# A gated mix of memory attention and FFN: the order of all five engines written in the source

## The chip, the cores and the metric

The kernel runs on one core of a Trainium2 chip. The metric is the time of one execution in microseconds on the device. The engines are named PE (TensorE), ACT (ScalarE), DVE (VectorE), POOL (GpSimd) and SP (SyncE, which here only starts transfers and signals).

## The reference

x is 2048 rows of 640 in float32. Attention has 32 heads of 20 channels and goes over four segments ("chunks") of 512 rows; from chunk to chunk it carries a memory M and its normaliser z. Beside it stands a gated FFN of width 1728, and a gate per row mixes the two.

```python
for s in range(4):
    logits = einsum("bhqd,bhkd->bhqk", qs, ks) * scale + causal_mask
    a_dot  = softmax(logits) @ vs
    pq     = phi(qs)                      # phi(t) = t + 1 if t > 0 else exp(t)
    a_mem  = (pq @ M) / (pq @ z + 1e-6)
    outs.append(g * a_mem + (1 - g) * a_dot)      # g = sigmoid(beta), per head
    M, z   = M + phi(ks).T @ vs, z + sum(phi(ks))
a = concat(outs) @ wo
b = (silu(x @ w1) * (x @ w3)) @ w2
out = sigmoid(x . gate_w) * a + (1 - sigmoid(x . gate_w)) * b
```

## The kernel before

Each float32 operand of a large product is split into a rounded high part and a low remainder, and a product is made of three passes (high by high, high by low, low by high). The split is a cast on ACT and a subtraction on POOL or DVE (`split`, L128; from PSUM `split_psum`, L326).

PE's work is a stream of *works* (`Work`, L132): the projections q, k, v (`q0_2` is chunk 0, block 2), the FFN's gate and up products g and u, its down product f (`f0_13_1_0`: chunk 0, group that begins with block 13, rows 1, columns 0), the output projection op, and the works of the memory: pkt (transposes of phi(k)), pm (the update of M), nd (the read). Every work is cut into two halves of its contraction, 64 rows each, that run on the two row halves of PE; the first halves form one stream and the second halves another, and `step` (L281) writes matmuls of the two alternately. The second half of a work starts behind a `nop` on SP that waits for its first half (`one`, L194, the wait is put down to L204). A work takes one of eight PSUM banks, and its `evac` writes the steps that empty the bank and go on from there.

Between these works the writer sets attention's steps, on slots (`attention`, L1042): `s_unit` (L850; scores, and their row maximum on DVE at L869), `max_rows` (L873), `t_unit` (L887; shifted scores, the exponential on ACT at L901, a triangle on POOL at L904) and `pv_quad` (L909). Tiles s, t, P and o belong to these.

The writer counts estimated PE time per half (`clocks`) and uses it for two things only: which half goes next, and when a bank is taken to be free again: a fixed `hold` after the work's last matmul (`close_work`, L189). A few steps are set by fixed distances: the transposes of phi(k) 3.4 us after their k work, the update of M 1.9 us after those (L663, L679). The FFN's down product may start as soon as the Python list `hts` has its inputs, which is when the chain's code was written, not when it is done.

The FFN's chain: g is read by a tanh on ACT (L757) and a product on DVE (L758); u by a product on DVE (L775); then ht is cast on ACT and its remainder taken on POOL (both in `split`, L129 and L130). f's result is folded into acc by ACT for the first group (L807) and by DVE afterwards (L809). Weights W come in by SP's DMA (L369) into raw tiles wr, a number of steps later their split is written (`w_split`, L373); its cast is pinned behind an exponential. X of chunks 2 and 3 is split by `split_x` (L478). oT is the transposed attention output, split for op (`part`, L1073).

Only PE and SP take the order of the source. The instructions of ACT, DVE and POOL are ordered by the framework's scheduler, which runs its own model of time, except where `here` keeps program order and `behind` pins an instruction behind another.

Of the kernel before, what the change touches and what calls it, by code (L numbers as in the profile page):

```python
# [18 lines left out]
P = 128  # L19
# [10 lines left out]
NP, AGE = 2, 4  # L30
# [7 lines left out]
STEP = 700  # L38


@with_exitstack
def gated_mix(ctx: ExitStack, tc: tile.TileContext, xT, wqk, wv, w13, w2, w2h, wo, beta, out):
# [40 lines left out]
    def gates():  # L83
        here(nc.sync.dma_start(gH, beta.rearrange("(o h) -> o h", o=1).broadcast_to([P, H])))
        for i in range(4):
            here(nc.sync.dma_start(cR[i::4], beta.rearrange("(h o) -> h o", o=1)))
        for g in (gH, cR):
            here(nc.scalar.activation(g, g, AF.Exp, scale=-1.0))
            here(nc.vector.tensor_scalar(g, g, 1.0, None, op0=ALU.add))

        nc.vector.reciprocal(cR, cR)
        nc.vector.tensor_scalar(cR, cR, -1.0, 1.0, op0=ALU.mult, op1=ALU.add)
# [16 lines left out]
    here = tc.keep_in_program_order  # L109
    last = {}  # L110

    def behind(ins):

        def pin(i):
            if ins is not None:
                tc.add_manual_dep(i.ins, ins.ins.name,
                                  mybir.DependencyInfo(mybir.DependencyClass.NoSync, mybir.DependencyReason.DATA),
                                  reason="behind")
            return i
        return pin  # L120
# [7 lines left out]
    def split(dst, src, lo=None, pin=lambda ins: ins):  # L128
        pin(nc.scalar.copy(dst[:, 0], src))  # L129
        (lo or nc.gpsimd.tensor_sub)(dst[:, 1], src, dst[:, 0].bitcast(F32))  # L130

    class Work:  # L132

        def __init__(self, name, parts, evac, hold, old=None, olds=None, ready=None):
            self.ready = ready
            self.name, self.parts, self.evac, self.hold, self.old, self.olds = name, parts, evac, hold, old, olds or {}
# [10 lines left out]
    def bank_tile(name, hold=1500):  # L147
# [28 lines left out]
    def open_work(w):  # L176

        k = until.index(min(until))
        until[k] = float("inf")
        w.bank = k  # L180
# [8 lines left out]
    def close_work(w):  # L189

        until[w.bank] = max(clocks) + w.hold
        w.evac(w.ps)
# [51 lines left out]
    def events():  # L244

        while dense["ns"] >= dense["hook"]:
            dense["hook"] += STEP
            stores()
            w_step()
            for f in on_step:  # L250
                f()
        for e in list(timed):
            if dense["ns"] >= e[0] and len(under) < 2 and len(behind_one) < 3:
# [63 lines left out]
    def finish_all():  # L317

        while flight[0] is not None or behind_one or under or timed or waiting:
            if flight[0] is None and behind_one:  # L320
                dense["n0"] += APART
            if step(None) is None:
                dense["ns"] += STEP
                events()

    def split_psum(dst, src, name, pin=lambda ins: ins):  # L326

        hi = bank_tile(name, 1800)[:, :src.shape[-1]]
        pin(nc.scalar.copy(dst[:, 0], src))
        nc.scalar.copy(hi, dst[:, 0].bitcast(F32))  # L330
        nc.vector.tensor_sub(dst[:, 1], src, hi)
# [27 lines left out]
    def w_load():  # L359
# [10 lines left out]
        raws.append([k, raw, n, clock["step"], None])  # L370
        clock["next"] += 1

    def w_split():  # L373
        k, raw, n, _, after = raws.pop(0)
        assert k < clock["oldest"] + NW
        w = sp.tile([P, 2, D + 2], FR, tag="W", name=f"W{k}", bufs=NW)
        tiles[k] = w
        if k not in EARLY:
            freed.append(clock["step"])
        split(w[:, :, :n], raw[:, :n], lo=nc.vector.tensor_sub if k < 7 else None, pin=behind(after))  # L380

    def w_step():


        clock["step"] += 1
        for r in raws:
            if clock["step"] - r[3] == (AGE // 2 if "exp" in last else 2 * AGE) and r[0] >= 7:
                r[4] = last.get("exp", last["act"])
# [3 lines left out]
        elif raws and raws[0][0] < clock["oldest"] + NW and \  # L392
                clock["step"] - raws[0][3] >= (AGE if "exp" in last or raws[0][0] < 7 else 2 * AGE + 1):
# [6 lines left out]
    def w_get(i):  # L400

        while i not in tiles:
            if not raws or raws[-1][0] < i and len(raws) < NRAW:
# [10 lines left out]
    def load_first(c):  # L414
# [21 lines left out]
        def hi(dst, src):  # L436
            last["act"] = here(nc.scalar.copy(dst[:, 0], src))
# [18 lines left out]
    def load_wide(c):  # L456
        for _ in EARLY:
            w_load()
        for kb in range(KB):
            split(Xs[c][:, :, kb, :], xraw[c][:, kb], lo=nc.vector.tensor_sub if kb % 2 else None)  # L460
# [17 lines left out]
    def split_x(c):  # L478
        x_tile(c)
        for kb in range(KB):  # L480
            split_psum(Xs[c][:, :, kb, :], xraw[c][kb], f"xh{c}_{kb}", here)
# [28 lines left out]
    def parts(name, ps, phi=None):  # L510


        s = ht_tile([P, 2, L], FR, name)
        last["act"] = nc.scalar.copy(s[:, 0], ps)
        if phi is not None:
            e = f_tile("phi_t")
            last["act"] = nc.scalar.activation(e, ps, AF.Relu, scale=-1.0)
            last["act"] = nc.scalar.activation(e, e, AF.Exp, scale=-1.0)
        nc.vector.tensor_sub(s[:, 1], ps, s[:, 0].bitcast(F32))
        if phi is not None:  # L520
            nc.vector.scalar_tensor_tensor(phi, ps, 0.0, e, op0=ALU.max, op1=ALU.add)
        return s
# [20 lines left out]
    def q_block(c, mb, i, alloc, oldest=None):  # L543

        def evac(ps):
            if c and mb == 0:
                big["q", c] = alloc(f"pq{c}")
            s = parts(f"qs{c}_{mb}", ps, big["q", c][:, mb * L:(mb + 1) * L] if c else None)
            store_parts(0, c, mb, s)
            q_done.add((c, mb))  # L550

        yield Work(f"q{c}_{mb}", proj(w_get(i), Xs[c]), evac, 2200, i if oldest is None else oldest)
# [805 lines left out]
```

## Time and profile before

| | us |
|---|---|
| median of three runs | 1167.65 (1167.01 to 1170.57) |
| the profiled run | 1166.93 |
| its span, first to last instruction | 1165.2 |
| PE busy | 1113.2 (96%) |
| DVE busy | 584.9 (50%) |
| POOL busy | 551.4 (47%) |
| ACT busy | 485.8 (42%) |
| mean granted clock of PE, as a share of full speed | 0.990 |

Times in rows are microseconds from the start of the span. "Idle before" and the name behind an arrow say how long an engine stood still ahead of an instruction and what ended it. The granted clock (PEclk) is 1.00 at PE's full level, 2.4 GHz, and 0.5 at its lower one, 1.2 GHz; a stretch with a mean between them spent part of its time at either.

### The profile page before, as it was taken

How to read it: one execution, taken by the hardware profiler on the slowest of the kernel's cores; microseconds unless marked ns; L12 is line 12 of the kernel's file. 1: busy time of each engine (PE TensorE's matmuls, PEld its weight loads, DVE VectorE, ACT ScalarE, POOL GpSimd, SP SyncE). 2: the span in 40 equal slices, each digit the busy share in tenths (PEclk: the TensorE clock that was granted, in tenths of full speed). 3: DMA queues.
4: the chain of work that ended last, by engine and by line, in shares of the span. 5: the costliest groups of instructions: out<-in, count | busy, mean ns of one | idle time of the engine just before them, and what ended most of it. 6: DMA issues, size and time to landing. Idle time of an engine off the chain costs nothing. (4 is left out here: it accounts for less than half of the span.)

```text
span 1165.2 us, 29806 instructions
## 1 busy us (share of the span) xinstructions
PE 1113.2 (96%) x11798; PEld 993.9 (85%) x11798; DVE 584.9 (50%) x1735; ACT 485.8 (42%) x1003; POOL 551.4 (47%) x739
## 2 busy tenths in 40 slices
PE   9999999999999999979999989988999999999998
PEld 6989988888988898869988767877898789887988
DVE  5032564355655644454344666763456774553644
ACT  5255334544352433344445634534443445245130
POOL 5344356455464545334344445643763647464230
PEclk9999999999999999989999999998999999999999
DMA  8355753334343323614477873425643434452111
GB/s 289 117 201 197 232 155 95 83 96 110 87 111 92 102 53 107 180 34 149 124 247 246 264 229 84 119 76 163 164 116 92 109 86 126 105 153 60 49 51 76
DMA packets 85883, 152.34 MB, mean 131 GB/s; under 512 B 19914, under 2 KB 33009, under 8 KB 85745
## 3 DMA queue, kind: packets, MB, share of 16 engines
q1 hardware_dynamic: 55569, 94.13, 25.2%
q0 software_dynamic: 22976, 41.90, 15.2%
q10 hardware_dynamic: 7200, 14.42, 3.4%
q8 instruction: 93, 1.52, 0.6%
q14 instruction: 45, 0.37, 0.1%
HBM read 94.92 MB, written 54.53 MB: 128 GB/s over the span
## 5 line engine op out<-in xcount | busy, mean ns | idle before, releaser
L201 PE MATMUL g<-X,W 64*128 64x512 f32 x1680 | 383.2, 397 | 2.5 <-SPq L204 1.7
L201 PE MATMUL u<-X,W 64*128 64x512 f32 x1560 | 363.6, 397 | 1.8 <-ACT P L901 1.0
L869 DVE CUSTOM_DVE_ANT_0 junk<-s,mask 128x128 bf16<-128x128 f32 (+3 forms) x512 | 250.5, 489 | 193.9 <-PE s L860 152.6
L201 PE MATMUL f<-W,ht 64*128 64x320 f32 x2624 | 281.5, 314 | 11.4 <-POOL ht L130 3.3
L130 POOL TENSOR_TENSOR W<-wr,W 128x640 fp32r<-128x640 f32 (+1 forms) x125 | 194.8, 1567 | 191.8 <-ACT W L129 161.9
L201 PEld LDWEIGHTS g<-X,W 64*128 64x128 f32 x1680 | 266.5, 186 | 14.4 <-SPq L204 2.1
L201 PEld LDWEIGHTS f<-W,ht 64*128 64x128 f32 x2624 | 259.0, 189 | 18.4 <-ACT ht L129 4.1
L201 PEld LDWEIGHTS u<-X,W 64*128 64x128 f32 x1560 | 253.7, 186 | 13.2 <-issue 2.0
L901 ACT ACTIVATE P<-t 128x384 f32<-128x384 f32 (+1 forms) x384 | 181.3, 527 | 183.2 <-PE t L896 176.1
L904 POOL TENSOR_SCALAR_AFFINE_SELECT P<-P 128x256 f32<-128x256 f32 (+1 forms) x192 | 95.0, 497 | 295.6 <-ACT P L901 260.7
L129 ACT CAST W<-wr 128x640 fp32r<-128x640 f32 (+1 forms) x130 | 91.8, 726 | 70.4 <-PE f L201 26.3
L896 PE MATMUL t<-qk 62*128 62x256 f32 (+2 forms) x512 | 97.3, 335 | 12.6 <-ACT acc L807 3.3
L201 PE MATMUL op<-W,oT 64*128 64x320 f32 x960 | 104.4, 310 | 2.0 <-DVE oT L130 1.9
L201 PE MATMUL k<-X,W 64*128 64x512 f32 x600 | 98.7, 402 | 0.0
L201 PEld LDWEIGHTS op<-W,oT 64*128 64x128 f32 x960 | 95.1, 185 | 4.3 <-DVE oT L130 3.3
L860 PE MATMUL s<-qk 60*128 60x256 f32 (+2 forms) x512 | 93.4, 332 | 4.5 <-DVE acc L809 2.0
L809 DVE SCALAR_TENSOR_TENSOR acc<-f,cgate,acc 128x320 f32<-128x320 f32 x128 | 69.4, 548 | 48.0 <-PE f L201 47.5
L201 PE MATMUL q<-X,W 64*128 64x512 f32 x540 | 88.6, 396 | 0.0
L130 POOL TENSOR_TENSOR ht<-ft,ht 128x512 fp32r<-128x512 f32 x52 | 67.2, 1292 | 44.3 <-ACT ht L129 44.1
L896 PEld LDWEIGHTS t<-qk 62*128 62x128 f32 x512 | 64.9, 185 | 23.5 <-ACT acc L807 4.8
L201 PE MATMUL v<-W,X 64*128 64x320 f32 (+1 forms) x960 | 82.7, 307 | 0.6 <-DVE acc L809 0.6
L201 PEld LDWEIGHTS k<-X,W 64*128 64x128 f32 x600 | 80.7, 187 | 2.2 <-issue 0.2
(117 smaller groups left out, 1310.3 us busy)
## 6 DMA issues: line engine op xcount, KB each, us to landing
qk<-qkd POOLq DMA_DIRECT2D x128, 240.0 KB, 4.2
wr<-in_w_dram SPq DMA_DIRECT2D x80, 320.0 KB
qkd<-qs SPq DMA_DIRECT2D x20, 512.0 KB
qkd<-ks SPq DMA_DIRECT2D x20, 512.0 KB
od<-oq ACTq DMA_DIRECT2D x32, 256.0 KB
wr<-in_wo_dram SPq DMA_DIRECT2D x20, 320.0 KB
vg<-vd SPq DMA_DIRECT2D x16, 336.0 KB
xr<-in_xT_dram SPq DMA_DIRECT2D x20, 256.0 KB
```

The lines of the kernel that those rows point to most:

```text
L129: pin(nc.scalar.copy(dst[:, 0], src))
L130: (lo or nc.gpsimd.tensor_sub)(dst[:, 1], src, dst[:, 0].bitcast(F32))
L201: ins = nc.tensor.matmul(o, l, x, start=i == 0 and (r == 0 or not w.todo[0]), stop=i == len(todo) - 1 and (r == 1 or not w.todo[1]), skip_ ...
L809: nc.vector.scalar_tensor_tensor(dst, ps[:, :320], cgate[:, c, lb:lb + 1], dst, op0=ALU.mult, op1=ALU.add)
L860: nc.tensor.matmul(ps[i][:, o:o + n], q[:, qb * P:(qb + 1) * P], k[:, :n], start=qb != 1, stop=qb != 0, skip_group_check=True)
L869: nc.vector.tensor_tensor_reduce(out=junk[:, :n], in0=ps[i][:, o:o + n], in1=mask[:, L - n:], scale=1.0, scalar=-3.0e38, op0=ALU.add, op1= ...
L896: nc.tensor.matmul(ps[i][:, o:o + L - q0], k[:, kb * P:(kb + 1) * P], q[:, q0:], start=kb != 2, stop=kb != 3, skip_group_check=True)
L901: last["exp"] = nc.scalar.activation(u["P"][:, i, o:o + n], ps[i][:, b:b + n], AF.Exp, scale=SCALE)
L904: nc.gpsimd.affine_select(d, d, pattern=[[0, 2], [0, n], [1, P]], base=0, channel_multiplier=-1, compare_op=ALU.is_ge, fill=0.0)
```

## The change

All five engines take the order of the source (`ENGINES`). `here` becomes empty, `behind` and the pins go. To make that order, the writer keeps a clock of estimated durations for ACT, DVE and POOL (`busy`), a heap of steps that are due at a time (`later`, `due`), and writes a chain step by step (`stages`): each step is written when the one before it is done by the clock. A bank is free when the chain's last reader is done by the clock, and PE's clock is moved on where it takes a bank that is not free yet (`take_bank`). `hts`, `tiles` (the weights), `q_done` and `ready` are set when the last step of a chain is written, so that works that ask for them come later. The row maxima, exponentials and triangles are steps of this kind as well. The transposes of phi(k) and the update of M follow the clock's end of their chain. A weight's split is written 6 steps after its load and not 4 (`AGE`). The gates' exponentials are written 6 us after beta's loads. The computation is the same, with the same matmuls.

```diff
-NP, AGE = 2, 4
+NP, AGE = 2, 6
+ENGINES = ("PE", "SP", "Activation", "DVE", "Pool")
...
-        for g in (gH, cR):
-            here(nc.scalar.activation(g, g, AF.Exp, scale=-1.0))
...
+        later(now() + 6000, lambda: stages(None, ("act", 400, powers), ("dve", 400, sums)))
...
-    here = tc.keep_in_program_order
...
+    busy, heap = dict(act=0.0, dve=0.0, pool=0.0), []
+
+    def now():
+        return max(clocks)
+
+    def go(e, ns, ready=0.0):
+
+        busy[e] = max(busy[e], now(), ready) + ns + 60
+        return busy[e]
+
+    def later(t, f):
+        heapq.heappush(heap, (t, len(order_of), f))
+        order_of.append(0)
...
+    def due():
+        while heap and heap[0][0] <= now():
+            heapq.heappop(heap)[2]()
+
+    def force():
+
+        clocks[:] = [max(c, heap[0][0]) for c in clocks]
+        heapq.heappop(heap)[2]()
+
+    def stages(bank, *todo):
+
+        def run(i):
+            e, ns, f = todo[i][:3]
+            t = go(e, ns)
+            if bank is not None and len(todo[i]) > 3:
+                until[bank] = t
+            if i + 1 < len(todo):
+                later(t, lambda: run(i + 1))
+            f()
+
+        run(0)
...
+    def take_bank():
+
+        while min(until) == float("inf"):
+            if heap:
+                force()
+            elif not lower():
+                raise RuntimeError("no bank")
         k = until.index(min(until))
-        until[k] = max(clocks) + hold
-        return pp.tile([P, L], F32, tag=f"b{k}", name=name, bufs=1)
+        clocks[:] = [max(c, until[k]) for c in clocks]
+        until[k] = float("inf")
+        return k
...
-        until[w.bank] = max(clocks) + w.hold
-        w.evac(w.ps)
+        w.evac(w.ps, w.bank)
...
     def w_step():
 
...
-        for r in raws:
-            if clock["step"] - r[3] == (AGE // 2 if "exp" in last else 2 * AGE) and r[0] >= 7:
-                r[4] = last.get("exp", last["act"])
...
+        elif raws and raws[0][0] < clock["oldest"] + NW and clock["step"] - raws[0][3] >= AGE:
             w_split()
...
-            if pk is not None:
-                timed.append((dense["ns"] + 3400, lambda: memory_turn(c, mb)))
...
+                  lambda: pk is not None and timed.append((busy["dve"] + 300, lambda: memory_turn(c, mb))))
...
-                nc.vector.scalar_tensor_tensor(t, u, 0.5, pu, op0=ALU.mult, op1=ALU.mult)
-                split(ht, t)
-                hts[c, j] = ht
+
+                def low():
+                    nc.gpsimd.tensor_sub(ht[:, 1], t, ht[:, 0].bitcast(F32))
+                    hts[c, j] = ht
+
+                stages(bank, ("dve", 690, lambda: nc.vector.scalar_tensor_tensor(t, u, 0.5, pu, op0=ALU.mult, op1=ALU.mult), True),
+                       ("act", 600, lambda: nc.scalar.copy(ht[:, 0], t)), ("pool", 1290, low))
...
+                until[bank] = go("act", 430) if first else go("dve", 545)
...
+        for i in range(2):
+            later(now() + 100 + i, lambda i=i: row_max(i))
```

Three places of the order follow. In these rows a tile's name ends in a number of its own, which differs between the two kernels; `128x147` is the output of both halves of a pass.

PE at the first update of M, before. The row of pm0_0 at the top is the last of its first half; the others of pm0_0 belong to its second half.

```order
L201 MATMUL pm0_0_1120<-V0_287,pkn0_0_1101 128x147
L201 MATMUL k1_1_1006<-X1_104,W8_365 128x512
L199 MATMUL pkt0_1_1135<-ident_84,pk0_1_1080 128x64 x2
L201 MATMUL k1_1_1006<-X1_104,W8_365 128x512
L199 MATMUL pkt0_1_1135<-ident_84,pk0_1_1080 128x64 x2
L199 MATMUL pkt1_0_1088<-ident_84,pk1_0_1017 128x64
L201 MATMUL k0_2_1075<-X0_102,W9_905 128x512
L199 MATMUL pkt1_0_1088<-ident_84,pk1_0_1017 128x64 x2
L201 MATMUL k0_2_1075<-X0_102,W9_905 128x512
L199 MATMUL pkt1_0_1088<-ident_84,pk1_0_1017 128x64
L201 MATMUL pm0_0_1120<-V0_287,pkn0_0_1101 128x147
```

The same place after: the first half's last row and what follows it, and, 28 rows behind the former, the start of the second half.

```order
L251 MATMUL pm0_0_1131<-V0_286,pkn0_0_1092 128x147
L251 MATMUL k0_2_1068<-X0_102,W9_905 128x512 x2
L249 MATMUL pkt0_1_1155<-ident_84,pk0_1_1074 128x64 x2
L251 MATMUL k0_2_1068<-X0_102,W9_905 128x512
L249 MATMUL pkt0_1_1155<-ident_84,pk0_1_1074 128x64 x2
L251 MATMUL k1_2_1126<-X1_104,W9_905 128x512
```

```order
L251 MATMUL pm1_0_1182<-V1_591,pkn1_0_1150 128x147
L251 MATMUL k0_2_1068<-X0_102,W9_905 128x512 x2
L251 MATMUL pm1_0_1182<-V1_591,pkn1_0_1150 128x147
L251 MATMUL k0_2_1068<-X0_102,W9_905 128x512
L251 MATMUL pm1_0_1182<-V1_591,pkn1_0_1150 128x147
L251 MATMUL k0_2_1068<-X0_102,W9_905 128x512
L251 MATMUL pm1_0_1182<-V1_591,pkn1_0_1150 128x147
L251 MATMUL pm0_0_1131<-V0_286,pkn0_0_1092 128x147
```

Between the two pieces stand k0_2 and k1_2 in turn. The distance from the first half's end to the second half's start went from 10 rows to 28.

PE at the FFN's last group for chunk 0, before. The first row is the last matmul of u0_12; ht0_12 is made from it, and f0_13_0_0 reads it in the last row.

```order
L201 MATMUL u0_12_7357<-X0_102,W58_6858 128x512
L201 MATMUL f0_13_0_0_7510<-W59_6924,ht0_13_7390 128x320
L201 MATMUL g1_13_7446<-X1_104,W56_6760 128x512
L201 MATMUL f0_13_0_0_7510<-W59_6924,ht0_13_7390 128x320
L201 MATMUL g1_13_7446<-X1_104,W56_6760 128x512
L201 MATMUL f0_13_0_0_7510<-W60_7331,ht0_12_7506 128x320 x2
```

After, the last matmul of u0_12 stands 41 rows ahead of the last row of this piece; g1_12, g1_13, u1_12 and one scores unit lie between.

```order
L251 MATMUL u1_12_7543<-X1_104,W58_6847 128x512
L251 MATMUL g1_12_7488<-X1_104,W57_6801 128x512
L1019 MATMUL t22_1_0_7561<-qk2_88 128x384
L1019 MATMUL t22_1_1_7562<-qk2_88 128x384
L251 MATMUL f0_13_0_0_7559<-W59_6946,ht0_13_7369 128x320
L251 MATMUL g1_12_7488<-X1_104,W57_6801 128x512
L251 MATMUL f0_13_0_0_7559<-W59_6946,ht0_13_7369 128x320
L251 MATMUL g1_12_7488<-X1_104,W57_6801 128x512
L251 MATMUL f0_13_0_0_7559<-W60_7331,ht0_12_7505 128x320 x2
```

f0_13_0_0 moved back behind the chain's clock.

ACT at the first down products of chunk 2, before. W92 and W93 are weights, acc2 the accumulator, oq38 the result of an attention quad, P40 an exponential.

```order
L129 CAST W92_11904<-wr92_11846 128x640
L807 ACTIVATE acc2_11694<-f2_0_0_0_11701,cgate_101 128x320
L807 ACTIVATE acc2_11694<-f2_0_0_1_11750,cgate_101 128x320
L129 CAST W93_11955<-wr93_11862 128x640
L807 ACTIVATE acc2_11694<-f2_0_1_0_11793,cgate_101 128x320
L919 COPY oq38_11925<-o38_11908 128x512
L921 DMA od2_78<-oq38_11925 128x512
L807 ACTIVATE acc2_11694<-f2_0_1_1_11825,cgate_101 128x320
L901 ACTIVATE P40_11968<-t40_0_0_11969 128x512
```

The same place after.

```order
L916 ACTIVATE acc2_11700<-f2_0_0_0_11701,cgate_101 128x320
L1026 ACTIVATE P39_11758<-t39_2_0_11848 128x384
L1026 ACTIVATE P39_11758<-t39_2_1_11849 128x384
L916 ACTIVATE acc2_11700<-f2_0_0_1_11741,cgate_101 128x320
L916 ACTIVATE acc2_11700<-f2_0_1_0_11787,cgate_101 128x320
L1057 COPY oq38_11936<-o38_11919 128x512
L1060 DMA od2_78<-oq38_11936 128x512
L916 ACTIVATE acc2_11700<-f2_0_1_1_11825,cgate_101 128x320
L171 CAST W92_11962<-wr92_11834 128x640
L171 CAST W93_11976<-wr93_11859 128x640
L1026 ACTIVATE P40_11980<-t40_0_0_11981 128x512
```

The two casts moved behind the four evacuations into acc2 and stand directly ahead of P40.

## Rows read from the trace of the kernel before

**Rows 1.** The page: busy time of the engines.

```profile
PE 1113.2 (96%) x11798; PEld 993.9 (85%) x11798; DVE 584.9 (50%) x1735; ACT 485.8 (42%) x1003; POOL 551.4 (47%) x739
```

**Rows 2.** Timeline of PE: start, length, engine, line, operation, count.

```profile
49.78 8.27 PE L201 MATMUL v<-W,X 64*128 64x320 f32 x110
...
62.02 7.63 PE L201 MATMUL k<-X,W 64*128 64x512 f32 x63
...
1157.67 2.37 PE L201 MATMUL op<-W,oT 64*128 64x320 f32 x15
```

**Rows 3.** Busy time by stretch: length, PE, PEld, DVE, ACT, POOL, PEclk, DMA share, GB/s.

```profile
75.00:87.00 12.00, 9.13 (x90) 8.45 (x89) 2.73 (x7) 4.22 (x11) 4.23 (x6) 0.86 0.71 229
140.00:475.00 335.00, 331.00 (x3531) 296.20 (x3529) 177.44 (x562) 136.39 (x277) 172.46 (x219) 1.00 0.37 99
475.00:532.00 57.00, 48.20 (x454) 41.87 (x452) 29.42 (x71) 22.96 (x43) 22.41 (x30) 0.94 0.38 118
582.00:586.00 4.00, 2.22 (x22) 1.64 (x20) 1.88 (x3) 2.66 (x5) 3.83 (x4) 1.00 0.67 215
640.00:726.00 86.00, 77.66 (x758) 64.45 (x756) 54.06 (x174) 40.64 (x84) 41.66 (x60) 1.00 0.65 199
766.00:815.00 49.00, 41.70 (x480) 37.61 (x478) 21.77 (x83) 20.03 (x43) 20.33 (x29) 0.93 0.37 113
815.00:1080.00 265.00, 256.85 (x2704) 221.51 (x2702) 144.52 (x469) 116.17 (x243) 151.38 (x206) 1.00 0.43 113
1080.00:1130.00 50.00, 46.53 (x511) 45.32 (x508) 26.55 (x46) 11.60 (x20) 14.05 (x12) 0.97 0.14 43
```

**Rows 4.** Timelines of SP and PE, 74 to 80 us.

```profile
74.34 2.55 SPq L86 DMA_DIRECT2D cR<-in_beta_dram  x4
77.51 1.91 SPq L506 DMA_DIRECT2D qkd<-ks  x2
...
80.12 0.39 PE L201 MATMUL pm<-V,pkn 64*128 64x147 f32 x1 [2.39 <-SPq L204]
```

**Rows 5.** Timelines of DVE, ACT, POOL and PE at f0_13_0_0.

```profile
496.54 0.69 DVE L775 SCALAR_TENSOR_TENSOR ft<-fu,u 128x512 f32<-128x512 f32 x1 [0.44 <-PE u L201]
...
497.64 0.61 ACT L129 CAST ht<-ft 128x512 fp32r<-128x512 f32 x1
...
498.34 1.27 POOL L130 TENSOR_TENSOR ht<-ft,ht 128x512 fp32r<-128x512 f32 x1 [4.08 <-ACT ht L129]
...
498.31 0.41 PE L201 MATMUL f<-W,ht 64*128 64x320 f32 x1 [1.41 <-ACT ht L129]
499.67 0.41 PE L201 MATMUL f<-W,ht 64*128 64x320 f32 x1 [0.80 <-POOL ht L130]
```

**Rows 6.** Timelines of ACT and PE, 789 to 797 us.

```profile
789.99 0.73 ACT L129 CAST W<-wr 128x640 fp32r<-128x640 f32 x1 [3.95 <-DMA wr<-in_w_dram]
794.49 0.72 ACT L129 CAST W<-wr 128x640 fp32r<-128x640 f32 x1 [2.93 <-DMA wr<-in_w_dram]
...
795.69 1.27 PE L896 MATMUL t<-qk 62*128 62x512 f32 x2 [2.92 <-ACT acc L807]
```

**Rows 7.** PE's waits (us in total, times, longest), and two in its timeline.

```profile
PE op L201 <- DVE oT L130: 1.9, 2, 1.4
PE g L201 <- SPq L204: 1.7, 1, 1.7
...
521.94 4.10 PE L201 MATMUL f<-W,ht 64*128 64x320 f32 x32 [1.60 <-POOL ht L130]
...
699.37 0.38 PE L896 MATMUL t<-qk 62*128 62x256 f32 x1 [1.90 <-DVE ft L775]
```

**Rows 8.** Timelines of DVE and POOL at an oT split, and oT's durations (least, median, longest).

```profile
390.22 4.38 DVE L130 TENSOR_TENSOR oT<-oall,oT 128x256 fp32r<-128x256 f32 x2 [0.47 <-ACT oT L129]
...
390.46 3.08 POOL L130 TENSOR_TENSOR W<-wr,W 128x640 fp32r<-128x640 f32 x2
...
L130 DVE TENSOR_TENSOR oT<-oall,oT x32: 407/546/3609, 390.2 to 1148.8; 128x256 fp32r<-128x256 f32 x16, 128x384 fp32r<-128x384 f32 x16
```

More of the change, by code (lines that the diff above doesn't have):

```diff
@@ L106, in selection, with here @@
             nc.gpsimd.tensor_add(sel[base:base + 3 * n, f0:f1], w[:, 0, o:o + f1 - f0], w[:, 2, o:o + f1 - f0])
-    here = tc.keep_in_program_order
[L110 to L120, printed above, removed]
+    def here(ins):
+        return ins
     def order(ins, behind):
@@ L252, in events @@
         for e in list(timed):
-            if dense["ns"] >= e[0] and len(under) < 2 and len(behind_one) < 3:
+            if now() >= e[0] and len(under) < 2 and len(behind_one) < 3:
                 timed.remove(e)
@@ L317, in finish_all @@
     def finish_all():
-        while flight[0] is not None or behind_one or under or timed or waiting:
+        while flight[0] is not None or behind_one or under or timed or waiting or heap:
             if flight[0] is None and behind_one:
@@ L369, in w_load, with done @@
         queue.dma_start(raw[:, :n], src)
-        raws.append([k, raw, n, clock["step"], None])
+        raws.append([k, raw, n, clock["step"]])
         clock["next"] += 1
     def w_split():
-        k, raw, n, _, after = raws.pop(0)
+        k, raw, n, _ = raws.pop(0)
         assert k < clock["oldest"] + NW
         w = sp.tile([P, 2, D + 2], FR, tag="W", name=f"W{k}", bufs=NW)
[L377 to L380, printed above, removed]
+        halfway.add(k)
+        def done():
+            tiles[k] = w
+            halfway.remove(k)
+            if k not in EARLY:
+                freed.append(clock["step"])
+        split(w[:, :, :n], raw[:, :n], k < 7, 730, done)
+    halfway = set()
     def w_step():
         clock["step"] += 1
-        for r in raws:
-            if clock["step"] - r[3] == (AGE // 2 if "exp" in last else 2 * AGE) and r[0] >= 7:
-                r[4] = last.get("exp", last["act"])
         if raws and raws[0][0] in EARLY:
@@ L436, in hi @@
         def hi(dst, src):
[L437 removed]
+            here(nc.scalar.copy(dst[:, 0], src))
         def lo(dst, src, eng=nc.vector):
@@ L557, in q_pair @@
         clock["oldest"] = i
-        ps = [bank_tile(f"q{c}_{mb}", 8000) for mb in range(2)]
+        banks, ps = zip(*[bank_tile(f"q{c}_{mb}") for mb in range(2)])
         hh, hl, lh = PASSES
@@ L853, in s_unit @@
         m = u["m"]
-        ps = [bank_tile(f"s{p}_{t}_{i}", 1300 + 500 * i) for i in range(2)]
+        todo = []
+        banks, ps = zip(*[bank_tile(f"s{p}_{t}_{i}") for i in range(2)])
         for qb in ((0, 1), (2,), (3,))[t]:
@@ L862, in s_unit, with row_max @@
                 put(i, n * COL)
-        for i in range(2):
+        def row_max(i):
             for qb in ((0, 1), (2,), (3,))[t]:
@@ L964, in load_memory @@
         while not all(("g", c, qb, hf) in stored for qb in range(4) for hf in range(2)):
+            yield 1
+        while c == 1 and read.count(2) < 8:
             yield 1
```

284 lines of the change are left out of this document (176 added, 108 removed).

## The prediction

> **What bounds the kernel now.** I read the page's busy line first [rows 1]: the matmul engine PE works through 1113.2 of 1165.2 us, and no other engine through more than 584.9. So the end is set by PE: by its work, by the pace at which it runs, and by its waits. The profiled run took 1166.93 us, 1.73 beyond its span and 0.72 under the median of the three runs, 1167.65; I make the sum against 1166.93 and take the result for the median as it stands, since the difference is under a thousandth.
>
> Pace next [rows 2]. PE runs two streams, one on each half of its rows. With both streams full, a matmul of 320 columns starts every 73 ns ((8.27 − 0.31) / 109, the 0.31 being the length of the last) and one of 512 every 117 ns ((7.63 − 0.39) / 62). With one stream alone a 320-column matmul starts every 147 ns ((2.37 − 0.31) / 14). A stretch in which one half has nothing to do therefore shows as busy at half the pace.
>
> Then the waits, place by place [rows 3]. Each row is a stretch; its length less the PE column is idle time, and one less the PEclk column, times the length, is what PE loses by running at 1.2 GHz, the lower of its two clock levels. The idle times of these stretches come to 44.7 us, most of the 52.0 that PE lacks over the span; the others are the start and the end. The clock adds 1.7 at 75 to 87, 3.4 at 475 to 532, 3.4 at 766 to 815 and 1.5 at 1080 to 1130: 10.0. It drops right behind an idle stretch each time, so a wait costs more than it lasts. Some 54.7 us are thus at stake among what the trace shows as waits, and they are spread: no single place is worth 1% of the span, apart from 475 to 532 with 12.2.
>
> **The change part by part.** PE's work is the same: the same matmuls, in an order that differs by some tens of places. What changes is (i) who orders the other three engines, and (ii) that the writer now follows each chain of steps on a clock, and puts a PE work into PE's order only when its last input has been written down.
>
> *The first memory works, 75 to 87.* PE waits 2.39 us for the nop on SP that lets the second half of pm0_0 start; SP was issuing four loads of beta (2.55 us) and two qkd stores (1.91 us) [rows 4]. In the old order ten rows lie between the halves, mostly small transposes; in the new one 28, mostly 512-column matmuls at 117 ns, some 2.5 us more of work. SP's loads stay where they are, so the same queue is there, but the wait is covered. Idle 2.87 and clock 1.7: I take −4.5, bounds 0 (SP's queue moves along) and −4.5.
>
> *The last FFN group, 475 to 532.* The chain from the last u0_12 matmul to f0_13_0_0 is a product on DVE (0.69 us), a cast on ACT (0.61, begun 0.41 late behind other work of ACT) and a subtraction on POOL (1.27) [rows 5]; it runs from 496.54 to 499.61, 3.1 us, and PE waits 1.41 for the cast and 0.80 for the subtraction. Before, four rows of PE lie between the two ends; after, 40, or 40 × 0.117 = 4.7 us when paired. This wait goes, and with it the waits for DVE that follow when both halves arrive late, and the SP wait of 1.7 us ahead of g, where PE was too far ahead in one half [rows 7]. I leave the twin of this place, f1_13_0_0 (1.60 us [rows 7], and 1.7, half of the clock's loss here): in the new order ht1_12's cast and subtraction still stand behind two weights on ACT and POOL. With 1.3 for new waits, 4.6 of the 12.2 stay and 7.6 go. Bounds: −9 and −2.
>
> *ACT behind late weights, 766 to 815.* ACT's order held the cast of W92 and W93 ahead of the evacuations of four output tiles. ACT stood 3.95 and 2.93 us at these casts, their data not there, and PE stood 2.92 us for a bank that ACT had not emptied [rows 6]; a slow stretch followed. In the new order all four evacuations are ahead of both casts, and the exponentials P40 behind. The idle time is 7.3 and the clock's loss 3.4. I take the 2.9, all of the clock, and 1.5 of the other 4.4, which are waits for DVE and one for a weight on POOL that stays: −7.8. If W93 is again as late as here, P40 waits instead; bounds −10.7 and −2.
>
> *582 to 586.* PE is idle for 1.78 us [rows 3], ahead of the transposes of pk2_0, since a fixed 3.4 us was allowed for its chain; now the transposes are written 0.3 us after the clock's end of that chain: −1.8, bounds 0 and −1.8.
>
> *640 to 726.* Here waits for DVE follow each other, the longest of 1.90 us for ft2 [rows 7]. DVE is busy 54.06 of 86 us, against half of the whole span [rows 1, 3]. A better order helps whom PE waits for, but DVE's work stays. I take half of the idle 8.34, −4.2 (bounds 0 and −8).
>
> *The rest.* 140 to 475 has 4.0 idle, 815 to 1080 8.15, 1080 to 1130 3.47 with 1.5 of clock. The same mechanisms, each wait of 1 us or so: waits for an evacuation go where the bank's end is now modelled; waits at the end of attention, around 1042 and 1071, stay, as little is left there to fill PE with. I take −2.2, −2.2 and −2.5.
>
> Gains: 4.5 + 7.6 + 7.8 + 1.8 + 4.2 + 2.2 + 2.2 + 2.5 = 32.8.
>
> *What it costs.* Works that wait for their inputs leave the other half alone. Counted in the order, PE has a matmul followed by another on the same half 583 times against 538. At 74 ns (147 − 73) to 117 ns each the 45 cost 3.3 to 5.3 us; I take 4.4. Waits on SP nops move with them. The gates' exponentials, mr's loads and the casts under no pin any more change places on queues that are idle half of the time (ACT 485.8, POOL 551.4 us busy of 1165.2 [rows 1]), so I cost them at nothing; if that cover fails, a load that is late costs about what W92 does now, 3 us.
>
> *What is not seen as idle.* The large forms (f, op and v with 320 columns, g, u, k and q with 512) are some 8,900 matmuls, half of each kind, and at paired pace need 4,540 × 0.073 + 4,380 × 0.117 = 844 us of the 1113 [rows 1, 2]; the rest holds scores, attention and memory works, and halves that wait alone. How much is the latter the rows don't say. If the waits shrink, this shrinks too; I take −8, a quarter of the visible gain, bounds 0 and −20.
>
> Sum: 1166.9 − 32.8 + 4.4 − 8 = 1130.5, so **1131 us**.
>
> *A rule that speaks against it.* On one occasion two DVE subtractions for oT took 4.38 us together, the longer 3.61, where their median is 0.55; POOL ran two weight subtractions of 1.5 us each over just that time [rows 8]. The new clocks for DVE and POOL know nothing of each other, so the new order may put these side by side more often. The Trainium skill, in "SBUF — State Buffer" under "SBUF: two separate sides", says that a DVE instruction with two SBUF inputs and a GpSimd one that reads SBUF take a shared port pair in turn, each holding it for its whole length. By that rule, the trace agrees, at 3.61 us. What it would cost here is the last rival.
>
> **The rivals.** *Half of it.* The clock's durations are round numbers (ACT 600, DVE 690 ns, all engines free of DMA waits and of semaphore time), and a wait that is covered at one place may appear at the next. Half of 32.8, all of the 4.4, nothing hidden: 1166.9 − 16.4 + 4.4 = 1155. For it: chains of DVE waits as at 640 to 726. Against it: the three largest places have distances in the new order that I can count.
>
> *No change.* PE's order is nearly the old one, and PE is 96% busy. If the framework's order of ACT, DVE and POOL was already as good, waits of 44.7 us stay, at 1167. Against it: at 766 to 815 the change of ACT's order is plain.
>
> *Slower: halves out of step.* The 45 extra one-half steps cost 3.3 to 5.3 us at once, while the waits may merely move from one cause to another. With no wait removed it ends at 1171 to 1172. It decides as soon as the waits removed sum to less than 4.4 us, fewer than the 75 to 87 stretch alone.
>
> *Slower: DVE behind POOL.* Each of the four chunks has two oT subtractions that PE can come to with no other work at hand, those of its first part. At the longest, each would be held for two POOL subtractions less its own time, 3.1 us [rows 8], 25 us in all; the lateness would reach PE only where no other work is left, as now (PE waited 1.9 us in two places for oT [rows 7]). Half of 25, 12 us, on top of the half case's 1155 is 1167, no change; only beside a gain of less than 8.5 us does it end slower, at 1170 to 1179.
>
> **How the numbers follow.** About 0.3%, 3.5 us, is what a measurement of this kernel can tell from no change. My forecast with its bounds (1108 to 1147) has 0.60; half of it (1147 to 1161) 0.22; a trace of a gain, 1161 to 1164, 0.03; no change 0.06; halves out of step 0.06; DVE behind POOL 0.03. Faster: 0.60 + 0.22 + 0.03 = 0.85; same 0.06; slower 0.09. For the range: the low end is the sum with the hidden part at −20 and the places 475 to 532, 640 to 726, 766 to 815 and the rest at or near their far bounds, −10 more, so 1108; the high end takes in the half case, 1161.
>
> **What would show it.** Right: PE's idle under 30 us; no PE wait for SP near 78 us; no wait of f0_13_0_0 for ht0_12; ACT's evacuations of acc2 run on without a pause and PE has no 2.9 us wait there; PEclk 1.00 in three of the four slow stretches. The wait for ht1_12 near f1_13_0_0 should still be there. Wrong: PE as busy as now but for longer (out of step), PE idle as now with other names behind it (moved), oT subtractions of 3 us beside POOL (port), or ACT casts of W that wait for DMA with exponentials behind them and PE's t works waiting for banks. I would be most wrong if the hidden part is zero and the DVE chains stay whole: 1166.9 − 32.8 + 5.4 + 4.4 = 1144.

## The result, and the profile after

The changed kernel takes 1136.98 us (1133.82 to 1137.45, three runs) against 1167.65; the ratio is 0.9723, with a 95% interval of 0.9686 to 0.976. The profiled run's span is 1135.7 us, 29.5 shorter. On the page, PE's busy time fell by 6.3 us, so 23.2 of the 29.5 are idle time; the other engines are as busy as in [rows 1]. The lines of the page: busy time, and the granted clock in 40 slices.

```profile
PE 1106.9 (97%) x11798; PEld 988.7 (87%) x11798; DVE 582.5 (51%) x1735; ACT 485.6 (43%) x1003; POOL 552.0 (49%) x739
...
PEclk9999999999999999999999999999999999999999
```

The same stretches as in [rows 3], bounded by nearly the same works of PE, so at earlier times (the counts of PE's matmuls in them differ by up to 25); one stretch (512 to 618) is wider here than the 582 to 586 of before. Columns as there.

```profile
73.00:84.00 11.00, 10.28 (x109) 9.54 (x107) 3.62 (x9) 6.34 (x14) 4.52 (x4) 1.00 0.65 211
134.00:462.00 328.00, 327.19 (x3524) 294.05 (x3523) 173.36 (x562) 135.12 (x276) 171.55 (x218) 1.00 0.39 104
462.00:512.00 50.00, 47.39 (x459) 41.20 (x457) 28.89 (x71) 22.62 (x43) 19.84 (x24) 0.97 0.37 117
512.00:618.00 106.00, 105.74 (x1196) 97.00 (x1196) 41.03 (x126) 53.76 (x118) 48.99 (x77) 1.00 0.61 198
618.00:706.00 88.00, 82.02 (x783) 72.12 (x780) 58.42 (x183) 42.36 (x87) 40.25 (x57) 0.96 0.65 202
747.00:788.00 41.00, 37.63 (x477) 34.40 (x475) 22.19 (x85) 19.25 (x43) 20.28 (x29) 1.00 0.48 140
788.00:1052.00 264.00, 260.02 (x2707) 220.34 (x2705) 145.07 (x470) 116.65 (x245) 150.94 (x205) 0.99 0.43 112
1052.00:1101.00 49.00, 45.95 (x514) 44.55 (x512) 26.14 (x47) 11.80 (x21) 13.85 (x12) 1.00 0.15 44
```

Worked out as in the prediction (length less PE, and one less PEclk times the length; for 788 to 1052 the clock's loss is 1.75, from a slice of 25 us at 0.93), idle and clock together went:

| place (before) | before | after | change | forecast |
|---|---|---|---|---|
| 75 to 87 | 4.6 | 0.7 | −3.9 | −4.5 |
| 140 to 475 | 4.0 | 0.8 | −3.2 | −2.2 |
| 475 to 532 | 12.2 | 4.1 | −8.1 | −7.6 |
| 582 to 586 and around | 2.0 | 0.3 | −1.7 | −1.8 |
| 640 to 726 | 8.3 | 9.5 | +1.2 | −4.2 |
| 766 to 815 | 10.7 | 3.4 | −7.3 | −7.8 |
| 815 to 1080 | 8.2 | 5.7 | −2.5 | −2.2 |
| 1080 to 1130 | 5.0 | 3.1 | −1.9 | −2.5 |
| sum | | | −27.4 | −32.8 |

The table leaves out 726 to 766 (after: 706 to 747), where the prediction had no term: PE is idle there 0.2 us before and 1.5 after.

The waits of PE that are left (us in total, times, longest):

```profile
PE t L1019 <- DVE m L981: 4.6, 5, 3.4
PE f L251 <- POOL ht L880: 3.4, 3, 2.2
PE rr L251 <- DMA rR<-rp: 2.3, 1, 2.3
PE op L251 <- DVE oT L167: 2.0, 4, 0.7
PE s L970 <- ACT P L1026: 1.8, 1, 1.8
```

The longest of before are gone: the SP nop at pm0_0, the bank behind ACT's casts, ht0_12. The 2.2 us for POOL's ht is ht1_12, which the prediction left standing.

Where ACT stood at late weights [rows 6], the timelines of ACT and PE now read:

```profile
771.52 0.72 ACT L171 CAST W<-wr 128x640 fp32r<-128x640 f32 x1
774.03 0.72 ACT L171 CAST W<-wr 128x640 fp32r<-128x640 f32 x1 [1.79 <-DMA wr<-in_w_dram]
774.66 1.08 ACT L1026 ACTIVATE P<-t 128x512 f32<-128x512 f32 x2
...
775.31 0.44 PE L970 MATMUL s<-qk 60*128 60x384 f32 x1 [1.76 <-ACT P L1026]
```

W93 is still late, but behind it stand the exponentials P40 and not the evacuations: PE loses 1.76 us and no slow stretch, where it lost 2.92 and one.

The place that got no better, 618 to 706, in the timelines of DVE, POOL and PE:

```profile
664.03 0.49 DVE L681 TENSOR_TENSOR gm<-nd,nd_r 128x320 f32<-128x320 f32 x1 [2.44 <-DMA gd<-gm]
...
667.56 0.49 DVE L681 TENSOR_TENSOR gm<-nd,nd_r 128x320 f32<-128x320 f32 x1 [2.08 <-DMA gd<-gm]
...
676.42 1.65 DVE L1087 TENSOR_TENSOR rs<-rs,rp 128x128 f32<-128x128 f32 x1
...
676.39 1.53 POOL L167 TENSOR_TENSOR W<-wr,W 128x640 fp32r<-128x640 f32 x1 [0.34 <-ACT W L171]
...
679.58 0.76 PE L1019 MATMUL t<-qk 62*128 62x256 f32 x3 [3.41 <-DVE m L981]
```

DVE, now in a fixed order, stops 2.44 and 2.08 us at two gm tiles whose last contents are still on their way to memory. Then chunk 1's scaling chain (reciprocal and five steps, 674.7 to 678.8) stands ahead of the row maxima of s35, whose bank t32 needs; one of its steps, 0.29 us elsewhere, takes 1.65 beside POOL's weight subtraction. PE waits 3.41 us, and 3.5 us more are lost at the lower clock behind it.

### The profile page after: what moved, and what is told of

Read it like the earlier page. It is cut to its first block, busy times and chain, and to the rows that moved or that the text cites. A ratio compares the mean times of both kernels' runs of the same rounds, so it can differ in the third digit from the quotient of the medians.

```text
span 1135.7 us, 29817 instructions
## 1 busy us (share of the span) xinstructions
PE 1106.9 (97%) x11798; PEld 988.7 (87%) x11798; DVE 582.5 (51%) x1735; ACT 485.6 (43%) x1003; POOL 552.0 (49%) x739
## 5 line engine op out<-in xcount | busy, mean ns | idle before, releaser
L251 PE MATMUL g<-X,W 64*128 64x512 f32 x1680 | 390.9, 397 | 0.1
L251 PE MATMUL u<-X,W 64*128 64x512 f32 x1560 | 373.9, 397 | 0.0
L251 PEld LDWEIGHTS g<-X,W 64*128 64x128 f32 x1680 | 271.9, 186 | 15.2 <-issue 2.0
L251 PE MATMUL f<-W,ht 64*128 64x320 f32 x2624 | 268.3, 311 | 5.0 <-POOL ht L880 3.4
L251 PEld LDWEIGHTS u<-X,W 64*128 64x128 f32 x1560 | 259.0, 187 | 14.4 <-issue 1.8
L251 PEld LDWEIGHTS f<-W,ht 64*128 64x128 f32 x2624 | 249.2, 187 | 10.4 <-POOL ht L880 5.1
L251 PE MATMUL op<-W,oT 64*128 64x320 f32 x960 | 99.6, 310 | 2.1 <-DVE oT L167 2.0
L251 PE MATMUL k<-X,W 64*128 64x512 f32 x600 | 95.9, 397 | 0.4 <-SPq L254 0.4
L251 PEld LDWEIGHTS op<-W,oT 64*128 64x128 f32 x960 | 91.2, 186 | 4.3 <-DVE oT L167 3.4
L1006 POOL DMA_DIRECT2D qk<-mr x128 | 73.5, 576 | 35.7 <-DVE mr L1000 30.4
```

The costliest lines, as they stand in the source:

```text
L251: ins = nc.tensor.matmul(o, l, x, start=i == 0 and (r == 0 or not w.todo[0]), stop=i == len(todo) - 1 and (r == 1 or not w.todo[1]), skip_ ...
L1006: after(3 + 9 * k + a, lambda d=dst, r=r: here(nc.gpsimd.dma_start(d, mr[r:r + 8])))
```

## The experiments

All are timed against runs of the kernel before on the same chip. They stood on three chips: e1 to e4 on one, e5, f1, f2 and the changed kernel run again on another, g1, h2, h3 and i1 on a third. The kernel before took 1166 to 1167 us on each; the changed one ran again on the second alone, at 1135.75, so a difference between runs of two chips is known to 1 or 2 us at best.

**Who orders the three engines.** Four kernels take the changed source, with PE's new order, and give some engines back to the framework. The old pins are gone in them too, so they say what PE's order is worth without the engines' order, not what a tuned mixture could give.

```diff
-ENGINES = ("PE", "SP", "Activation", "DVE", "Pool")
+ENGINES = ("PE", "SP")                    # e1_pe_sp
+ENGINES = ("PE", "SP", "Activation")      # e2_act
+ENGINES = ("PE", "SP", "DVE")             # e3_dve
+ENGINES = ("PE", "SP", "Pool")            # e4_pool
```

> The changed source, but only PE and SP take its order; ACT, DVE and POOL are ordered by the framework's scheduler again, without the old pins. Theory: the gain of 30.7 us has two parts of like size, the new places of PE's works (75 to 87, 475 to 532) and the order of the three engines (766 to 815, and short waits in between); then this ends near 1152. Rival 1, PE's order carries it all: 1137 to 1142. Rival 2, the order of the three engines carries it all: 1162 to 1170.

> As e1_pe_sp, but ACT takes the source's order as well; DVE and POOL are the framework's. Theory: ACT's share is the stretch of the late weights, some 6 us, and the evacuations it gives early: 1145, 7 below e1_pe_sp. Rival: the engines' orders only work together, and one alone in the source's order waits for the two others: not below e1_pe_sp.

> As e1_pe_sp, but DVE takes the source's order as well; ACT and POOL are the framework's. Theory: most of PE's waits before were for DVE, but the longest DVE wait after is of the source's own making (3.4 us behind the scaling chain of chunk 1): 1148, 4 below e1_pe_sp. Rival: not below e1_pe_sp.

> As e1_pe_sp, but POOL takes the source's order as well; ACT and DVE are the framework's. Theory: POOL's order decides only a few PE waits (ht remainders, 3.3 us before and 3.4 after): within 3 us of e1_pe_sp, near 1151. Rival: POOL in the source's order waits for ACT casts that the framework sets later: above e1_pe_sp.

Measured: e1_pe_sp 1188.65 us (ratio to before 1.0188, 1.0148 to 1.0228), e2_act 1165.58 (1.0001, 0.9981 to 1.0021), e3_dve 1169.04 (1.0026, 1.0005 to 1.0047), e4_pool 1181.63 (1.0125, 1.0081 to 1.017). All four expectations were off, e1's by the most: PE's new order, with the framework's order for the other three and without the old pins, is not half the gain but a loss of 22 us. Part of the reason can be read from PE's line on the page of e1_pe_sp and its waits:

```profile
PE 1127.8 (95%) x11798; PEld 1000.7 (84%) x11798; DVE 588.0 (50%) x1735; ACT 486.0 (41%) x1003; POOL 549.1 (46%) x739
...
PE t L1019 <- DVE m L981: 5.3, 7, 3.0
PE pm L251 <- ACT pkn L764: 5.0, 2, 2.6
PE rr L251 <- DMA rR<-rp: 3.8, 2, 2.3
PE pkt L249 <- DVE pk L598: 3.6, 2, 1.8
```

The memory works pkt and pm are now written 0.3 us behind the clock's end of their chains. In the old kernel the fixed distances allowed for an ACT and a DVE that might be late. With the framework's order those engines are late (pm waits 2.6 us for pkn), and a margin is missing. That is one named cause, 8.6 us in these rows (pm and pkt), but not the main one: e3_dve's PE still waits 3.6 us for each of the two, and is 19.6 us faster. e1_pe_sp's span is 22.2 us longer than before: 7.6 are idle time and 14.6 busy time of PE. The clock is 0.980 there, against 0.990 before, which makes some 12 of the latter (0.020 × 1187.4 less 0.010 × 1165.2). The other waits are spread over all three engines, and how much of the loss is owed to the lost pins and kept orders no run shows. From e1, ACT's order is worth 23.1 us, DVE's 19.6, POOL's 7.0; the sum, 49.7, is close to the 51 to 53 that all three give together. So the rival that the orders only work together falls: what the engines' orders give adds up. But all of it is needed before the plan is ahead by 2.7%.

**A fixed order without the plan.** The kernel before, all five engines in its source's order:

```diff
-    here = tc.keep_in_program_order
+    here = lambda ins: ins
...
-            if ins is not None:
-                tc.add_manual_dep(i.ins, ins.ins.name,
...
-tc.manual_schedule(engines={_mybir.EngineType.PE, _mybir.EngineType.SP})
+tc.manual_schedule(engines={_mybir.EngineType.PE, _mybir.EngineType.SP, _mybir.EngineType.Activation, _mybir.EngineType.DVE, _mybir.EngineType.Pool})
```

> The kernel before with one edit: all five engines take its source's order, in which each chain stands in one piece right behind the work's last matmul (the pins and kept orders have no meaning then and are gone). Theory: writing a chain's steps at their times is what makes a fixed order good; in one piece the steps of one chain hold up those of others on the three in-order engines, and this is slower than before: 1190 to 1250. Rival: any fixed order of the source is as good as the framework's, and this is within 10 us of 1167.

1172.04 us (1.0044, 1.0028 to 1.0061): 5 us slower, and the theory's 1190 to 1250 was wrong; the rival holds. Chains in one piece are a poor order, but not much poorer than the framework's. The first row of PE's waits shows its longest: pm for pkn, 7.5 us at one place.

```profile
PE pm L197 <- ACT pkn L672: 7.5, 1, 7.5
PE s L856 <- DVE acc L805: 4.9, 4, 3.6
```

**The plan for PE, but chains in one piece.** The middle step between the last kernel and the changed one.

```diff
     def stages(bank, *todo):
 
-        def run(i):
-            e, ns, f = todo[i][:3]
-            t = go(e, ns)
...
+        t = 0.0
+        for step_ in todo:
+            e, ns, f = step_[:3]
+            start = t
+            t = go(e, ns, t)
...
-            if i + 1 < len(todo):
-                later(t, lambda: run(i + 1))
             f()
+            said, flags[:] = flags[:], []
+            for g in said:
+                later(start, g)
```

> The changed kernel with one edit: the chains of splits, of the FFN and of q and k are written in one piece at their start, on all engines in the source's order; only the flags that let PE's works be written (ht, weights, oT, products) and the bank times still follow the clock. Attention's row maxima, exponentials and triangles keep their own times. Theory: a step that is written long before its input is there stops an in-order engine with all behind it, so the steps' places carry the gain, and this ends at 1155 to 1172, where the old kernel with its chains in one piece ended. Rival: what counts is that PE's works are written only once their inputs are planned to be there; the engines have slack enough for chains in one piece, and this ends at 1136 to 1144.

1154.19 us (0.991, 0.9879 to 0.9942), 0.8 below the theory's lower end of 1155 and by far outside the rival's. But the theory is only half right, since this is also 18 us less than e5_before_five, whose chains are in one piece too. So the gain over that kernel has two parts: some 18 us (1172 to 1154) come with the rest of the changed source, which holds PE's works at their planned readiness and the bank times, and also attention's row maxima, exponentials and triangles at their own times; another 18 (1154 to 1136) come from writing each step of a chain at its time. The kernels stand on two chips; by their ratios to the kernel before, the parts are 1.3% (16 us) and 1.7 to 1.9% (20 to 22 us), so they are of like size only roughly. What the readiness alone is worth in the first part, without attention's own times, no run shows. What the steps' places are worth is seen in g1_lumps' largest wait, and in the timelines of POOL and PE at its longest:

```profile
PE o L1052 <- POOL P L1035: 15.3, 11, 3.1
...
921.39 1.55 POOL L173 TENSOR_TENSOR W<-wr,W 128x640 fp32r<-128x640 f32 x1 [4.77 <-ACT W L177]
...
925.15 1.27 POOL L880 TENSOR_TENSOR ht<-ft,ht 128x512 fp32r<-128x512 f32 x1
926.37 1.02 POOL L1035 TENSOR_SCALAR_AFFINE_SELECT P<-P 128x256 f32<-128x256 f32 x2
...
926.85 1.55 PE L1052 MATMUL o<-P,vg 128*32 128x384 f32 x14 [3.13 <-POOL P L1035]
```

POOL's subtraction for a weight was written with its cast, and POOL stands 4.77 us until ACT has come to that cast; the triangle of P, whose exponential is done at 922.08, stands behind it, four DMA issues (2.2 us) and an ht, and the attention quad waits for it. In the changed kernel no quad waits for POOL.

**The clock's rule for banks.**

```diff
         k = until.index(min(until))
-        clocks[:] = [max(c, until[k]) for c in clocks]
         until[k] = float("inf")
```

> The changed kernel with one line less: taking a bank no longer moves PE's clock on to the time at which the bank is free. Theory: PE's clock then runs ahead of the chip wherever banks are short, steps are written too early against PE's works, and waits return where scores and FFN share the banks: 5 to 12 us slower, 1141 to 1148. Rival: banks are seldom short by the clock, and this is within 2 us of 1136.

1142.1 us (0.9802, 0.9772 to 0.9832), 6 us more than the changed kernel, as the theory had it in size. Its trace doesn't settle the reason: one wait of PE, of 7.7 us from 672 on, for gm, in the stretch that differs from run to run (below), makes up the loss in it.

**AGE.**

```diff
-NP, AGE = 2, 6
+NP, AGE = 2, 4
```

> The changed kernel with AGE back at 4 steps of 700 ns: weights' casts are written 1.4 us earlier by the clock. Theory: loads that land late (6 to 8 us beside others) now stop ACT at a cast more often, with exponentials and evacuations behind: ACT's waits for wr rise from 6.4 us to 12 or more, and the time by 3 to 8 us, 1140 to 1145. Rival: the place of four late loads is set elsewhere and AGE has no part in the gain: within 2 us of 1137.

1135.4 us (0.9726, 0.9694 to 0.9757): no difference, the rival holds for the time. ACT's waits for wr did rise, to 10.2 us against 5.8 in the changed kernel's second trace, and the wait of before came back in part. In the timelines of ACT and PE of f2_age4 the casts of W92 and W93 stand ahead of an evacuation again:

```profile
766.30 0.73 ACT L171 CAST W<-wr 128x640 fp32r<-128x640 f32 x1 [2.29 <-DMA wr<-in_w_dram]
771.02 0.72 ACT L171 CAST W<-wr 128x640 fp32r<-128x640 f32 x1 [4.00 <-DMA wr<-in_w_dram]
771.66 0.52 ACT L916 ACTIVATE acc<-f,cgate 128x320 f32<-128x320 f32 x1
...
772.23 0.97 PE L1019 MATMUL t<-qk 62*128 62x512 f32 x2 [1.67 <-ACT acc L916]
```

The stretch 747 to 788 loses 5.1 us of idle time and 1.6 at the lower clock there, against 3.4 in the changed kernel. This was the slowest of f2_age4's four executions (1139.8 us); the median doesn't show it.

**The stretch that got no better.** Chunk 1's scaling chain behind the row maxima, and the changed kernel again beside it:

```diff
-        here(nc.vector.reciprocal(rs, rs))
...
+        def lump():
+            nc.vector.reciprocal(rs, rs)
...
+            less = 2 if c == 1 else 0
...
+                    after((3 + 2 * i if end else 3 + 2 * i + k) - less,
...
+        if c == 1:
+            later(now() + 2600, lump)
+        else:
+            lump()
```

The chain of chunk 1 is written 2.6 us later, and its six transfers two of PE's steps (`less`) nearer behind it.

> The changed kernel with one edit: chunk 1's scaling chain on DVE (six steps, 674.7 to 678.8 in the trace) is written 2.6 us later, behind the row maxima that PE's t32 works wait for. Theory: the 3.4 us wait and the slow stretch behind it (3.5 us lost) are of this chain's place alone: 6 to 7 us go, 1130. Rival: DVE is the bound of this stretch, the wait reappears behind other row maxima or gm: within 2 us of 1137.

> The changed kernel itself once more, on the same chip as the runs beside it: 1134 to 1138 by every theory; it gives the measure for differences of a few microseconds.

f1_scale_later 1137.44 us (0.9751, 0.9717 to 0.9785), the changed kernel 1135.75 (0.9738, 0.9705 to 0.977). The 3.4 us for the row maxima are gone, yet the time is the same: the theory falls. In f1_scale_later's timelines of SP and PE the wait has another name:

```profile
675.44 5.22 SPq L1099 DMA_DIRECT2D rR<-rp  x6
...
679.83 0.79 PE L251 MATMUL g<-X,W 64*128 64x512 f32 x1 [4.11 <-SPq L254]
```

The six transfers of rR wait on SP for the chain, are then issued in a row for 5.2 us, and the nop that lets PE's second half start stands behind them. In the changed kernel they are issued in a row as well (676.41, 5.43 us). In the second trace of the changed kernel, too, the 3.4 us wait is not there; DVE stood still for 4.80 us at one gm tile instead, where the first trace has 2.44 at this tile and 2.08 at the next:

```profile
670.05 0.49 DVE L681 TENSOR_TENSOR gm<-nd,nd_r 128x320 f32<-128x320 f32 x1 [4.80 <-DMA gd<-gm]
```

So the wait in this stretch moves from tile to tile and from engine to engine, and the loss stays: in 618 to 706, PE is idle for 6.0 us in the changed kernel's first trace, 6.3 in its second and 6.3 in f1_scale_later, at a mean clock of 0.96 in each. More than one engine is late in it.

**Trying to take the rest.** Two versions aim at the waits that are left. `held` counts the last ht of a chunk while it is being made; no weight is split in that time.

```diff
 # h2_hold_skip
-        elif raws and raws[0][0] < clock["oldest"] + NW and clock["step"] - raws[0][3] >= AGE:
+        elif raws and raws[0][0] < clock["oldest"] + NW and clock["step"] - raws[0][3] >= AGE and not held[0]:
...
+                held[0] += j == NF - 1
...
+                    held[0] -= j == NF - 1
...
-    tail = [braid(chain([d] + u + [d2]), o1, 1500, 10500), alternate(o2, d3)]
+    tail = [braid(chain([d] + u + [d2]), o1, 1500, 13000), alternate(o2, d3)]
 # h3_all: these, lump as above, and
-                store_later(gd[c][:, qb, 320 * hf:320 * hf + 320], gm, ("g", c, qb, hf), n=4)
+                store_later(gd[c][:, qb, 320 * hf:320 * hf + 320], gm, ("g", c, qb, hf), n=3)
...
-                queue = nc.gpsimd if end and k else nc.sync
+                queue = nc.gpsimd if k else nc.sync
```

> The changed kernel with two edits: no weight split is written while an ht of FFN block 12 is under way, and chunk 3's normalisation starts 2.5 us later by the clock. Theory: the wait for ht1_12 (2.2 us, with 1.7 us of slow clock behind it) is of the two weights ahead of it on POOL and goes, and the wait for rR at the end (1.8 to 2.3 us) is covered by FFN works: 5 to 6 us, 1130. Rival: the waits move to the weights that come later or to the end: 1134 to 1138.

> h2_hold_skip with three more edits for 660 to 690 us: chunk 1's scaling chain 2.6 us later as in f1_scale_later, every second transfer of rR on POOL's queue and not on SP's, and gm stored 0.7 us sooner. Theory: the wait there was first DVE's place (3.4 us), then SP's six transfers in a row (4.1 us) with a nop behind; with both eased it goes with its slow stretch: 6 to 7 us below h2_hold_skip, 1124. Rival: DVE is the bound of this stretch and the wait takes a third name: within 2 us of h2_hold_skip.

h2_hold_skip 1135.77 us (0.9756, 0.9724 to 0.9787), h3_all 1131.73 (0.9719, 0.9687 to 0.975). The first did take its waits away: in its trace the stretch 462 to 512 is idle for 1.4 us at full clock, where it lost 4.1, and PE waits for rR no more. But in the same trace t waits 4.5 us for gm and 2.8 for row maxima later on, so the rival describes the time, though not the place it named. h3_all is lowest in its median by some 4 us, but its interval overlaps the changed kernel's, so a better version is not shown. Its trace tells why not more came of it. The stretch 640 to 706 has no wait over 1.6 us; but chunk 2's scaling chain met POOL, in the timelines of DVE, POOL and PE:

```profile
868.91 5.55 DVE L1092 TENSOR_TENSOR rp<-rs,rp 128x128 bf16<-128x128 f32 x1
...
869.19 1.54 POOL L167 TENSOR_TENSOR W<-wr,W 128x640 fp32r<-128x640 f32 x1
871.27 3.03 POOL L167 TENSOR_TENSOR W<-wr,W 128x640 fp32r<-128x640 f32 x2
...
875.28 0.76 PE L1021 MATMUL t<-qk 62*128 62x256 f32 x3 [5.48 <-DVE m L983]
```

A step of 0.29 us takes 5.55, over the length of three weight subtractions on POOL, and PE waits 5.48 for the row maxima behind it. That POOL held the step is read from their times; no run takes the subtractions away. POOL issues two transfers of rR there, 0.59 us each, one just ahead of the first subtraction and one behind it; h3_all itself put these on POOL's queue.

## Why the prediction was right, point by point

**The time** came out at 1137.0 for 1131, inside the range. The step that failed is one term: 640 to 726, put at −4.2 and measured at +1.2. That is 5.4 us, and the difference between 32.8 and 27.4 in the table. Of it, idle time fell by 2.4 us (8.3 to 6.0) where 4.2 were forecast, and 3.5 us at the lower clock came in addition, which the prediction had put at nothing. The working there took the wait of 1.90 us for ft2 [rows 7] as one for DVE's work, which a better order would ease, and did not ask what stood ahead of ft2 on DVE. That was the scaling chain of chunk 1, itself waiting for a transfer, in the timeline of DVE of the kernel before:

```profile
696.27 0.95 DVE L945 RECIPROCAL rs<-rs 128x128 f32<-128x128 f32 x1 [1.92 <-DMA rs<-od]
```

The change doesn't take this chain apart and leaves it ahead of the same row maxima of s35, so the wait stayed, under another name; and the gm tiles' stores, which DVE waits for, were left out. The other seven terms are within 1 us each. That the prediction's last line also holds a 5.4, which is worked out nowhere, is chance. Three small figures of it are off, and the forecast rests on none: 1166.9 and 3.3 to 5.3 make 1170 to 1172; 3.61 less 0.55 is 3.1, but two POOL subtractions (3.08) less 0.55 are 2.5; and the 1147 of its bounds has no sum behind it.

**The signs.** PE's idle is 28.8 us, under 30; the wait for SP near 78 is gone; PEclk is 1.00 in three of the four slow stretches. One sign of being wrong showed too: ACT's cast waits 1.79 us for its weight with exponentials behind it, and PE 1.76 for those. It cost little, since no bank hung on it.

**475 to 532, 75 to 87 and 766 to 815** went as argued, by distances counted in the order: f0_13_0_0 waits no more, pm0_0's nop is covered, the evacuations are ahead of the casts. That the rest at f1_13_0_0 stays was right as well (2.25 us for 1.60); h2_hold_skip shows that two weights on POOL were its cause.

**What it costs and what is not seen.** PE's busy time fell by 6.3 us. The clock accounts for 3.3 of it (10.0 lost before, 6.75 after), so 3 are net of the works' changed pairing; the forecast was +4.4 − 8 = −3.6. The two terms were not measured apart, and either could be wrong by as much as the other, so the nearness of the net bears out neither.

**Half of it and no change** did not come. That the framework's order was about as good as a fixed order in one piece is what e5_before_five shows (5 us), so the premise of "no change" was nearer than its chance of 0.06 says: without the steps' own times, the gain is 0.9%.

**Halves out of step** didn't decide, as the waits did go. **DVE behind POOL** was placed wrongly but is a mechanism that bites: oT's longest subtraction fell from 3.61 to 2.48 us, and the scaling chain was stretched by 1.4 us in the changed kernel and by 5.3 in h3_all. The Trainium skill, "SBUF — State Buffer", "SBUF: two separate sides", says that of a DVE instruction with two SBUF inputs and a GpSimd one that reads SBUF, the one that starts first has the shared port pair for its whole length. The trace of the changed kernel agrees, at 1.65 us beside a subtraction of 1.53. In h3_all's it differs: the DVE step began first by the trace (868.91 against 869.19) and still took as long as three subtractions; there the measurement stands.

**The reason** in the prediction, that PE is written at planned readiness and so its waits are covered, is about half of the cause at most by the runs. It took the order of the three engines as a help at one place (766 to 815); e1_pe_sp shows that PE's new order is a loss without it (there the old pins are gone too), and g1_lumps that chain steps written at their times are worth about as much as all the rest, 18 of the 36 us that lie between e5_before_five and the changed kernel.

## What to carry to other kernels

If one engine's order is planned on a clock, the engines that feed it have to follow the same clock: here a plan with small margins for PE and the framework's order for the rest, without the pins that order had, was slower than either (1188.65 us, against 1167 and 1136). Write each step of a chain at its planned time and not with the chain: on an in-order engine a step written early stops the finished work of others behind it. Look for what the plan leaves in one piece or takes as free (a scaling chain, transfers issued in a row, a store that a tile waits for, two engines that hold each other up): the waits that stayed were there, and in 618 to 706 the loss stayed when one of them was taken away.

## What the runs showed of the hardware

The granted clock also fell where PE's row names no wait of more than 0.33 us. In the changed kernel the last attention quad ran for 4.79 us instead of 2.36; before it stands a stretch with few matmuls (16 in 3.5 us, weights loading for 1.58), busy by the trace. This busy time holds small waits: eight t matmuls take 2.52 us there, where the eight before them took 0.82, and by the rows of weight loads each waits 0.20 to 0.54 us for one of ACT's exponentials. Windows of PE there, columns as in [rows 3]:

```profile
1040.00:1043.50 3.50, 3.11 (x16) 1.58 (x13) 0.00 (x0) 3.23 (x8) 1.39 (x3) 1.00 0.32 90
1043.50:1048.30 4.80, 4.78 (x34) 2.15 (x34) 0.00 (x0) 1.90 (x5) 1.57 (x4) 0.64 0.24 88
```

So a stretch of few matmuls, started one by one, was followed by the 1.2 GHz level without a long idle stretch. And a DVE step of 0.29 us can be held for the length of several POOL instructions, 5.55 us in h3_all.
